# Setting-up moved into the first attention, k ahead of q, output tiles by halves, a bank of its own for the first MLP tile

## Chip, core and metric

One core of one Trainium2 chip. The metric is the time of one execution on the device in microseconds (us), lower is better. An execution's time is its span (first to last instruction, as the profile gives it) plus about 2.0 us. An execution is called fast or slow by its clock and its distance from the fastest; only fast ones are compared. Every execution leaves its span and its mean granted TensorE clock; a full trace is kept of one execution per run.

## The reference

```python
B, H, S, D = 8, 8, 576, 64            # batches, heads, sequence, head width
# attention, per batch and head, two parts that are added:
#   coarse: q, k, v averaged over groups of 4 positions, softmax attention, each row repeated 4 times
#   local:  softmax attention with the mask |i - j| < 4
# x = attention output as (B*S, H*D) = (4608, 512)
h = x @ w_in                          # w_in (512, 2048)
g = 0.5 * h * (1.0 + erf(h / sqrt(2)))
out = g @ w_out                       # w_out (2048, 512), out float32 (4608, 512)
```

## The kernel before

One stream of work per engine: attention of batch 0 in a form of its own (a hand-made order of short steps), then for each of nine chunks of 512 tokens the first MLP product (`m1`), the second (`m2`), and between the second's matmuls the attention of the next batch. `mm()` gives the two PSUM banks `mm0` and `mm1` in turn.

```python
    def load_qk(b):
        for nm, src in (("qn", q), ("kn", k)):
            for c in range(NCK):
                nc.gpsimd.dma_start(
                    out=nat6(ld[b % 2][nm])[:, c, :, :],
                    in_=src[b, :, CH * c:CH * c + CH, :].rearrange("h s d -> s h d"))
                yield
# ... (cut)
    def m1(c):
        g = wpool.tile([128, NJ, 512], F16, tag="gT", bufs=2, name="gT")
        gT[c] = g
        x0 = 512 * c % XR
        if c:
            t = ppool.tile([128, 1024], F32, tag="nm", name="m_first")
            half = [t[:, 0:512], t[:, 512:1024]]
        else:
            half = [mm(), mm()]
        for fcs in ((0, 1, 2), (3,)):
            for j in range(2):
                for fc in fcs:
                    nc.tensor.matmul(out=half[j], lhsT=w_in_sb[:, fc, 128 * j:128 * j + 128],
                                     rhs=xT[:, fc, x0:x0 + 512], start=(fc == 0), stop=(fc == 3))
                    if fc == 3 and c == 0:
                        nc.scalar.activation(out=g[:, j, :], in_=half[j], func=ACTF.Gelu)
                    elif fc == 3 and j == 1:
                        nc.scalar.activation(out=g[:, 0:2, :], in_=t.rearrange("p (j c) -> p j c", j=2), func=ACTF.Gelu)
                    yield
        for j in range(2, NJ):
            ps = mm()
            for fc in range(4):
                nc.tensor.matmul(out=ps, lhsT=w_in_sb[:, fc, 128 * j:128 * j + 128],
                                 rhs=xT[:, fc, x0:x0 + 512], start=(fc == 0), stop=(fc == 3))
                if fc == 3:
                    nc.scalar.activation(out=g[:, j, :], in_=ps, func=ACTF.Gelu)
                yield
# ... m2: for each of four output tiles, 16 matmuls into ps = mm(), then a copy and a store (cut)
    def attn(b, fill):
        fill(6)
        scores(b, 0)
        s_lo(b)
        fill(6)
        mask(0)
        for p in range(NP):
            if p + 1 < NP:
                scores(b, p + 1)
                mask(p + 1)
                fill(2)
            else:
                fill(4)
            av(b, p)
            norm_out(b, p)
            if p + 1 == NP:
                to_gelu()
            else:
                fill(9)
# ... (cut): the attention of batch 0, from the list PLAN0; k, q and v of batch 0 go before all this
    run(load_qk(1))
    vg_load(1, v[1])
    vw_last(1, v[1])
    for f in range(4):
        nc.gpsimd.dma_start(out=w_out_sb[:, 4 * f:4 * f + 4, :],
                            in_=moe_w_out[512 * f:512 * f + 512, :].rearrange("(j p) c -> p j c", p=128))
        vw_load(1, v[1], [f])
    run(load_qk(2))
    first.close()
    ppool = ctx.enter_context(tc.tile_pool(name="psn", bufs=1, space=bass.MemoryType.PSUM, reuse_waits="tile"))
    for i in range(2):
        nc.vector.memset(ld[i]["vd"], 4.0)
        nc.vector.tensor_scalar(out=ld[i]["vlm"][:, :, 64:128], in0=maskL.unsqueeze(2).broadcast_to([128, H, 64]),
                                scalar1=4.0, scalar2=None, op0=ALU.mult)
# ... ON2, BH and ten copies that make `band` (cut)
    for c in range(NCH):
        b = c + 1
        f1 = filler(m1(c)) if c else f1_0
        if b <= 2:
            f1(10)
            for p in range(NP):
                t_in_g(b, p, "k")
                f1(7)
                t_in_g(b, p, "q")
                f1(4)
            k_lo()
            v_down(b)
        if b == 1:
            nc.vector.memset(ld[0]["vw"].rearrange("p j a d -> p (j a d)").bitcast(F32), 0.0)
            v_load(2)
            qk_cast(3)
        elif 2 < b < B:
            prep(b)
        f1()
# ... (cut)
```

The softmax here doesn't subtract the row's maximum and nothing guards it: scores larger than these inputs give would overflow.

Of the kernel before, what the change touches and what calls it, by code (L numbers as in the profile page):

```python
# [9 lines left out]
F32 = mybir.dt.float32  # L10
ACTF = mybir.ActivationFunctionType
ALU = mybir.AluOpType
# [4 lines left out]
def kernel(  # L17
# [9 lines left out]
    nc = tc.nc  # L27
    B, H, S, D = q.shape
    Sd = S // 4
    d_ff = moe_w_in.shape[1]  # L30
    NP = H // 2
# [59 lines left out]
    vlm0 = cpool.tile([128, H, 65], F16, tag="vlm0", name="v_lm0")  # L91
    Gb = cpool.tile([128, 240], F16, tag="Gb", name="Gb")
    GL = cpool.tile([128, 8, 16], F16, tag="GL", name="GL")
    dum = cpool.tile([128, 2], F32, tag="dum", name="dum")
    B0 = cpool.tile([128, 128], F16, tag="B0", name="B0")
    nb = cpool.tile([128, 128], F16, tag="nb", name="nb")
# [10 lines left out]
    def mm():  # L107
        turn[0] ^= 1
        return bank(turn[0])
# [7 lines left out]


    def load_qk(b):
        for nm, src in (("qn", q), ("kn", k)):  # L120
            for c in range(NCK):
                nc.gpsimd.dma_start(  # L122
                    out=nat6(ld[b % 2][nm])[:, c, :, :],
                    in_=src[b, :, CH * c:CH * c + CH, :].rearrange("h s d -> s h d"))
                yield
# [14 lines left out]
    def vg_load(b, src):  # L140
        L = ld[b % 2]
        nc.gpsimd.dma_start(out=L["vt"].rearrange("p h r d -> p h (r d)"),  # L142
                      in_=src[:, 0:512, :].rearrange("h (p r) d -> p h (r d)", r=4))
        nc.gpsimd.dma_start(out=L["vl"].rearrange("p r d -> p (r d)"),
                      in_=src[:, 512:576, :].rearrange("h (p r) d -> h p (r d)", r=4))
# [34 lines left out]
    for t in (kb.rearrange("p a j c -> p (a j c)"), ld[1]["vw"].rearrange("p j a d -> p (j a d)")):  # L180
        nc.scalar.copy(out=t.bitcast(F32).rearrange("p (n c) -> p n c", c=256),
                       in_=zt.bitcast(F32).unsqueeze(1).broadcast_to([128, 10, 256]))
    nc.vector.memset(B0, 1.0)
    nc.vector.memset(Gb, 1.0)
    nc.vector.memset(U, 1.0)
# [41 lines left out]
# [5 lines that stand above are left out]
            t = ppool.tile([128, 1024], F32, tag="nm", name="m_first")  # L232
            half = [t[:, 0:512], t[:, 512:1024]]
        else:
            half = [mm(), mm()]
        for fcs in ((0, 1, 2), (3,)):
            for j in range(2):
                for fc in fcs:
# [15 lines that stand above are left out]

    def m2(c):
        g = gT[c]
        for t in range(4):
            r0 = 512 * c + 128 * t
            if c == NCH - 1 and t == 3:
                for half in range(2):  # L260
                    cs = slice(256 * half, 256 * half + 256)
                    ps = mm()
                    for j in range(NJ):
                        nc.tensor.matmul(out=ps[:, 0:256], lhsT=g[:, j, 128 * t:128 * t + 128],  # L264
                                         rhs=w_out_sb[:, j, cs], start=(j == 0), stop=(j == NJ - 1))
                        yield
                    osb = wpool.tile([128, 512], F32, tag="osb", bufs=5, name="out_sb")[:, 0:256]
                    nc.vector.tensor_copy(out=osb, in_=ps[:, 0:256])  # L268
                    nc.sync.dma_start(out=out[r0:r0 + 128, cs], in_=osb)
                continue  # L270
            ps = mm()
            for j in range(NJ):
                nc.tensor.matmul(out=ps, lhsT=g[:, j, 128 * t:128 * t + 128],  # L273
                                 rhs=w_out_sb[:, j, :], start=(j == 0), stop=(j == NJ - 1))
                if j == NJ - 1:
                    osb = wpool.tile([128, 512], F32, tag="osb", bufs=5, name="out_sb")
                    (nc.vector.tensor_copy if c < NCH - 2 and t < 2 else nc.scalar.copy)(out=osb, in_=ps)  # L277
                    nc.sync.dma_start(out=out[r0:r0 + 128, :], in_=osb)
                yield
# [281 lines left out]
    def spin(n):  # L561
        ps = ppool.tile([128, 512], F32, tag="tr", name="spin")
        for _ in range(n):
            nc.tensor.matmul(out=ps, lhsT=zt[:, 0:128], rhs=zt, start=True, stop=True)



    PLAN0 = """
        Rk0:D Tk0:mm0 Rq0:D Tq0:mm1 KZ10:A NB Rk1:D QD0:A KD00:D QT0:A spin2 Tk1:av Rq1:D KD10:D Tq1:mm1
        KD01:A KZ00:A KZ01:D QT1:A spin1 S0:sc Rk3:D QD1:A Rk2:D KZ11:A Rq3:D Tk2:mm0 E10 KD11:D Tk3:mm1  # L570
        KD12:D E00 KZ12:D E20 Tq3:av KD13:D S1:sc KZ02:A QD3:D Rq2:D KD03:A QT3:D KD02:A E11 Tq2:mm0 KL
        VD:av E21 QD2:D QT2:D E01 S2:sc VLM VDe:A KZ03:D SL:mm0 EL KZ13:D E02 spin2 AV0:av E12 NA0
        AV1:mm0+mm1 E22 spin1 S3:sc NA1 TO0:av E13 XT0:D E23 AV2:mm0+mm1 E03 gelu NA2 TO1:av AV3:sc
        XT1:A NA3 spin1 TO2:av XT2:A spin3 TO3:sc M1A XT3:D M1B
    """
    spin(14)
    f1_0 = filler(m1(0))
    L0 = ld[0]
    slot = {}
# [17 lines left out]
    for word in PLAN0.split():  # L597
# [5 lines left out]
        elif nm == "NB":  # L603
            nc.vector.tensor_scalar(out=nb, in0=B0, scalar1=1.0, scalar2=30000.0,
                                    op0=ALU.subtract, op1=ALU.mult)
        elif nm == "gelu":
            to_gelu()
        elif nm[:2] == "M1":
# [57 lines left out]
            cp(out=xT[:, p, 0:512], in_=half[0])  # L666
            cp(out=xT[:, p, 512:576], in_=half[1][:, 0:64])
    run(load_qk(1))
    vg_load(1, v[1])
    vw_last(1, v[1])  # L670
    for f in range(4):
        nc.gpsimd.dma_start(out=w_out_sb[:, 4 * f:4 * f + 4, :],
                            in_=moe_w_out[512 * f:512 * f + 512, :].rearrange("(j p) c -> p j c", p=128))
        vw_load(1, v[1], [f])
    run(load_qk(2))
    first.close()
    ppool = ctx.enter_context(tc.tile_pool(name="psn", bufs=1, space=bass.MemoryType.PSUM, reuse_waits="tile"))
    for i in range(2):
        nc.vector.memset(ld[i]["vd"], 4.0)
        nc.vector.tensor_scalar(out=ld[i]["vlm"][:, :, 64:128], in0=maskL.unsqueeze(2).broadcast_to([128, H, 64]),  # L680
                                scalar1=4.0, scalar2=None, op0=ALU.mult)
    for hh in range(2):
        r = slice(64 * hh, 64 * hh + 64)
        nc.vector.memset(ON2[r, 64 * hh:64 * hh + 64], 1.0)
        nc.vector.memset(ON2[r, 64 - 64 * hh:128 - 64 * hh], 0.0)
        nc.vector.tensor_copy(out=BH[r, :], in_=B0[r, 64 * hh:64 * hh + 64])
    for j in range(NW):
        x = QN[j] - WN[j]
        nc.vector.tensor_copy(out=band[:, QN[j]:QN[j] + QL[j]], in_=BH[:, x:x + QL[j]])

    for c in range(NCH):
        b = c + 1
        f1 = filler(m1(c)) if c else f1_0
        if b <= 2:
            f1(10)
            for p in range(NP):
                t_in_g(b, p, "k")
                f1(7)
                t_in_g(b, p, "q")
                f1(4)  # L700
            k_lo()
            v_down(b)
        if b == 1:
            nc.vector.memset(ld[0]["vw"].rearrange("p j a d -> p (j a d)").bitcast(F32), 0.0)  # L704
            v_load(2)
            qk_cast(3)
        elif 2 < b < B:
            prep(b)
        f1()
        f2 = filler(m2(c))  # L710
        if b < B:
            to_exp()
            attn(b, f2)
            if b + 2 < B:
                v_load(b + 2)
            if b + 3 < B:
                qk_cast(b + 3)
        f2()
        if b + 2 < B:
            qk_turn(b + 2)  # L720
# [30 lines left out]
```

## Time and profile before

| | before |
|---|---|
| time, four executions | 331.18, 332.15, 329.6, 331.71 us |
| profiled execution: span, granted clock | 330.3 us, 0.995 |
| TensorE (PE) busy | 97% of the span |

The page's rows of busy tenths, 40 slices of 8.26 us each; a 9 is 90% or more:

```profile
PE   8988897999999999999999999999999999999996
DVE  7877677657847944799579957946793660000001
ACT  8745456775688778867886788678868886424710
```

PE loses time only in the first seven slices, which hold the attention of batch 0, the first MLP chunk and the attention of batch 1. The lines that carry the rest are in the prediction below. Two more rows, of the vector engine's (DVE's) timeline, are what the change is to move; the columns are start, length, engine, line, operation, output<-input, shape, count:

```profile
30.52 0.91 DVE L679 MEMSET v_d<- 128x1024 f16 x1 [0.16 <-issue]
53.37 2.19 DVE L704 MEMSET v_win<- 128x2560 f32 x1 [0.48 <-issue]
```

The first opens 4.5 us of setting-up between attention 0 and the first copies of k of batch 1. The second stands ahead of the first mask of batch 1.

### The profile page before, as it was taken

The page shows a single profiled execution, that of the slowest core. Times are in us where ns is not written, and L with a number is a line of the kernel's source. Part 1 is how long each engine was busy: PE and PEld are TensorE (multiplying, and loading weights), DVE is VectorE, ACT ScalarE, POOL GpSimd, SP SyncE. Part 2 cuts the span into 40 slices and gives each one's busy share as a digit, 9 for nine tenths or more (in the row PEclk, how much of TensorE's full clock was granted, in tenths as well). Part 3 has the DMA queues.
Part 4 walks back from the last instruction along what each step waited for, and adds up shares of the span by engine and source line. Part 5 has one row for each costly group of instructions (what it writes and reads, how often), then busy time and mean ns, then how long its engine had stood idle before and what let it go on. Part 6 is the DMA issues. An engine that isn't in the chain of part 4 may idle for free.

```text
span 330.3 us, 6291 instructions
## 1 busy us (share of the span) xinstructions
PE 319.2 (97%) x2526; PEld 172.7 (52%) x2526; DVE 198.5 (60%) x414; ACT 222.6 (67%) x395; POOL 121.7 (37%) x152
## 2 busy tenths in 40 slices
PE   8988897999999999999999999999999999999996
PEld 4864454545565445544554465446545654444444
DVE  7877677657847944799579957946793660000001
ACT  8745456775688778867886788678868886424710
POOL 8966766968372290293039303500000000000000
PEclk9999998999999999999999999999999999999999
DMA  6999999999999999999939994990100010011012
GB/s 82 163 201 156 151 190 160 145 194 145 168 124 192 207 151 154 202 145 172 168 83 129 158 171 113 133 113 32 65 32 0 34 65 32 0 66 64 0 50 80
DMA packets 150973, 38.76 MB, mean 117 GB/s; under 512 B 132896, under 2 KB 146464, under 8 KB 150944
## 3 DMA queue, kind: packets, MB, share of 16 engines
q0 software_dynamic: 122256, 23.02, 86.3%
q1 hardware_dynamic: 28688, 15.34, 22.5%
q8 instruction: 20, 0.33, 0.4%
q14 instruction: 9, 0.07, 0.1%
HBM read 46.01 MB, written 15.34 MB: 186 GB/s over the span
## 4 chain that ended last, share of the span: by engine, by line
PE 86%; POOL 5%; DMA 5%; DVE 2%; issue 1%; POOLq 0%; DVEq 0%
PE m_ps L273 36%; PE m_ps L249 32%; PE m_first L239 4%; DMA w_in_sb<-in_moe_w_in_dram 3%; PE nm L408 3%; PE sc L380 2%; PE sc L398 2%; DMA k_nat<-in_k_dram 1%; POOL old L174 1%; PE nm L405 1%; PE nm L404 1%; PE m_ps L264 1%; PE sc L376 1%; POOL k_nat L122 1%; POOL k_nat L168 1%; DVE v_win L704 1%
## 5 line engine op out<-in xcount | busy, mean ns | idle before, releaser
L273 PE MATMUL m_ps<-w_out_sb,gT 128*128 128x512 f16 x560 | 132.1, 380 | 1.8 <-DMA w_out_sb<-in_moe_w_out_dram 1.8
L249 PE MATMUL m_ps<-xT,w_in_sb 128*128 128x512 f16 x504 | 113.0, 379 | 0.5 <-ACT gT L242 0.5
L252 ACT ACTIVATE gT<-m_ps 128x512 f16<-128x512 f32 x126 | 75.2, 597 | 40.2 <-PE m_ps L249 40.2
L273 PEld LDWEIGHTS <-gT 128*128 128x128 f16 x560 | 51.3, 98 | 55.5 <-issue 3.0
L249 PEld LDWEIGHTS <-w_in_sb 128*128 128x128 f16 x504 | 48.0, 97 | 56.6 <-issue 1.8
L132 POOL DMA_DIRECT2D v_win<-in_v_dram x56 | 44.0, 824 | 19.3 <-DMA v_grp<-in_v_dram 10.0
L423 DVE TENSOR_TENSOR xl<-nm,lr 128x576 f16<-128x576 f32 x28 | 21.2, 758 | 27.0 <-ACT lr L419 27.0
L268 DVE COPY out_sb<-m_ps 128x256 f32<-128x256 f32 x2 | 0.8, 425 | 54.8 <-PE m_ps L264 54.8
L277 ACT COPY out_sb<-m_ps 128x512 f32<-128x512 f32 x21 | 12.3, 586 | 25.1 <-PE m_ps L273 24.9
L392 DVE TENSOR_TENSOR e<-e,band 128x576 f16<-128x576 f16 x28 | 12.5, 450 | 26.6 <-ACT e L387 26.6
L137 POOL DMA_DIRECT2D v_win<-in_v_dram x14 | 9.8, 787 | 48.0 <-PE nm L408 47.6
L435 DVE TENSOR_TENSOR xT<-xl,up 128x576 f16<-128x576 f16 (+8 forms) x41 | 22.1, 566 | 1.0
L417 ACT ACTIVATE lr<-sc 128x576 f32<-128x576 f32 x28 | 18.4, 658 | 2.5 <-PE sc L398 2.5
L418 ACT ACTIVATE lr<-lr 128x576 f32<-128x576 f32 x28 | 19.1, 683 | 0.9
L386 ACT ACTIVATE ed<-sc 128x288 f16<-128x288 f32 x28 | 11.4, 406 | 11.4 <-PE sc L380 11.4
L387 ACT ACTIVATE e<-sc 128x576 f16<-128x576 f32 x28 | 18.0, 644 | 0.0
L425 DVE TENSOR_TENSOR up<-nm,lr 64x144 f16<-64x144 f32 x56 | 16.5, 295 | 0.4
L239 PE MATMUL m_first<-xT,w_in_sb 128*128 128x512 f16 x64 | 15.1, 379 | 0.0
L244 ACT ACTIVATE gT<-m_first 128x1024 f16<-128x1024 f32 x8 | 8.2, 1024 | 8.7 <-PE m_first L239 8.7
L155 POOL DMA_DIRECT2D q<-in_q_dram x5 | 13.9, 2782 | 0.0
L142 POOL DMA_DIRECT2D v_grp<-in_v_dram x7 | 9.5, 1351 | 10.9 <-DVE v_two L350 10.9
L420 ACT ACTIVATE lr<-lr 64x288 f32<-64x288 f32 x28 | 12.4, 443 | 0.9
(186 smaller groups left out, 470.5 us busy)
## 6 DMA issues: line engine op xcount, KB each, us to landing
out_dram<-out_sb SPq DMA_DIRECT2D x35, 256.0 KB, 2.4
v_win<-in_v_dram POOLq DMA_DIRECT2D x56, 72.0 KB, 8.0
v_grp<-in_v_dram POOLq DMA_DIRECT2D x7, 512.0 KB, 11.1
k<-in_k_dram POOLq DMA_DIRECT2D x5, 576.0 KB, 12.5
q<-in_q_dram POOLq DMA_DIRECT2D x5, 576.0 KB, 15.0
w_in_sb<-in_moe_w_in_dram POOLq DMA_DIRECT2D x4, 512.0 KB, 8.6
w_out_sb<-in_moe_w_out_dram POOLq DMA_DIRECT2D x4, 512.0 KB, 9.5
q_nat<-in_q_dram POOLq DMA_DIRECT2D x12, 96.0 KB, 8.4
```

The source lines that it names most:

```text
L132: nc.gpsimd.dma_start(out=vw[64 * hh:64 * hh + 64, 0:9, p, 64 * hh:64 * hh + 64], in_=bass.AP(x.tensor, x.offset, [[D, 64], [57 * D, 9], [ ...
L155: nc.gpsimd.dma_start(out=t, in_=src[b].rearrange("h s d -> s h d"))
L239: nc.tensor.matmul(out=half[j], lhsT=w_in_sb[:, fc, 128 * j:128 * j + 128], rhs=xT[:, fc, x0:x0 + 512], start=(fc == 0), stop=(fc == 3))
L249: nc.tensor.matmul(out=ps, lhsT=w_in_sb[:, fc, 128 * j:128 * j + 128], rhs=xT[:, fc, x0:x0 + 512], start=(fc == 0), stop=(fc == 3))
L252: nc.scalar.activation(out=g[:, j, :], in_=ps, func=ACTF.Gelu)
L273: nc.tensor.matmul(out=ps, lhsT=g[:, j, 128 * t:128 * t + 128], rhs=w_out_sb[:, j, :], start=(j == 0), stop=(j == NJ - 1))
L387: nc.scalar.activation(out=e.rearrange("p (g c) -> p g c", g=2), in_=sc2[:, :, 0:SH], func=ACTF.Exp, scale=0.125)
L417: nc.scalar.activation(out=lr2, in_=sc2[:, :, 0:SH], func=ACTF.Ln)
L418: nc.scalar.activation(out=lr2, in_=lr2, func=ACTF.Exp, scale=-1.0)
L423: nc.vector.tensor_tensor(out=xl.rearrange("p (g c) -> p g c", g=2), in0=nm2[:, :, 0:SH], in1=lr2, op=ALU.mult)
L425: nc.vector.tensor_tensor(out=up[64 * hh:64 * hh + 64, :], in0=nm2[0:64, hh, SH:SH + Sd], in1=lrd[:, Sd * hh:Sd * hh + Sd], op=ALU.mult)
L435: nc.vector.tensor_tensor(out=xT[:, p, y:y + z - a].rearrange("p (g r) -> p g r", r=4), in0=xl[:, a:z].rearrange("p (g r) -> p g r", r=4), ...
```

## The change

The intent: take work and waits out of the stretch from 29 to 72 us. k of batch 1 is loaded and turned before q; constants are made in gaps of attention 0; the first MLP tile no longer shares a bank with the third; the first two output tiles are each summed in two halves, so that the last quarters of `w_out` are wanted later, and `w_out` is put earlier among the loads. The words `I0` to `I5` in the list PLAN0 are the moved pieces of setting-up. The core of the diff (cut: the tile `four` and its memset, the dispatch of the `I` words, the body of `warm`):

```diff
     def load_qk(b):
-        for nm, src in (("qn", q), ("kn", k)):
+        for nm, src in (("kn", k), ("qn", q)):
             for c in range(NCK):
@@ m1 @@
-            half = [mm(), mm()]
+            half = [ppool.tile([128, 512], F32, tag="tr", name="m_first"), mm()]
@@ m2 @@
     def m2(c):
         g = gT[c]
+        pair = [mm(), mm()] if c == 0 else []
+        if c == 0:
+            for t in range(2):
+                for j in range(NJ // 2):
+                    nc.tensor.matmul(out=pair[t], lhsT=g[:, j, 128 * t:128 * t + 128],
+                                     rhs=w_out_sb[:, j, :], start=(j == 0), stop=False)
+                    yield
         for t in range(4):
             r0 = 512 * c + 128 * t
-            ps = mm()
-            for j in range(NJ):
+            ps = pair.pop(0) if pair else mm()
+            for j in range(NJ // 2 if c == 0 and t < 2 else 0, NJ):
@@ attention 0 @@
+    def init(i):
+        if i < 2:
+            L = ld[1 - i]
+            nc.scalar.copy(out=L["vd"][:, :, 64:128], in_=four.unsqueeze(2).broadcast_to([128, H, 64]))
+            nc.scalar.activation(out=L["vlm"][:, :, 64:128], in_=maskL.unsqueeze(2).broadcast_to([128, H, 64]),
+                                 func=ACTF.Copy, scale=4.0)
+        elif i < 4:
+            t = ld[0]["vw"][:, 5 * i - 10:5 * i - 5].rearrange("p j a d -> p (j a d)")
+            nc.scalar.copy(out=t.bitcast(F32).rearrange("p (n c) -> p n c", c=256),
+                           in_=zt.bitcast(F32).unsqueeze(1).broadcast_to([128, 5, 256]))
+        elif i == 4:
+            for hh in range(2):
+                r = slice(64 * hh, 64 * hh + 64)
+                nc.vector.memset(ON2[r, 64 * hh:64 * hh + 64], 1.0)
+                nc.vector.memset(ON2[r, 64 - 64 * hh:128 - 64 * hh], 0.0)
+                nc.vector.tensor_copy(out=BH[r, :], in_=B0[r, 64 * hh:64 * hh + 64])
+        else:
+            for j in range(NW):
+                x = QN[j] - WN[j]
+                nc.vector.tensor_copy(out=band[:, QN[j]:QN[j] + QL[j]], in_=BH[:, x:x + QL[j]])
@@ PLAN0, the lines with an I word as they are after @@
+        KD01:A KZ00:A KZ01:D QT1:A spin1 S0:sc Rk3:D QD1:A Rk2:D KZ11:A Rq3:D Tk2:mm0 E10 I4 KD11:D Tk3:mm1
+        KD12:D E00 KZ12:D E20 I0 Tq3:av KD13:D S1:sc KZ02:A QD3:D Rq2:D KD03:A QT3:D KD02:A E11 Tq2:mm0 KL
+        VD:av E21 I1 QD2:D QT2:D E01 S2:sc VLM VDe:A KZ03:D SL:mm0 EL KZ13:D E02 spin2 AV0:av E12 NA0
+        AV1:mm0+mm1 E22 I2 spin1 S3:sc NA1 TO0:av E13 XT0:D E23 AV2:mm0+mm1 E03 gelu NA2 TO1:av AV3:sc
+        XT1:A NA3 I5 spin1 TO2:av XT2:A I3 spin3 TO3:sc M1A XT3:D M1B
-    spin(14)
+    spin(10)
+    warm()          # 40 small matmuls on zeros, into a bank of their own
@@ loads and set-up after attention 0 @@
-    vg_load(1, v[1])
-    vw_last(1, v[1])
     for f in range(4):
         nc.gpsimd.dma_start(out=w_out_sb[:, 4 * f:4 * f + 4, :],
                             in_=moe_w_out[512 * f:512 * f + 512, :].rearrange("(j p) c -> p j c", p=128))
-        vw_load(1, v[1], [f])
+        if f == 0:
+            vg_load(1, v[1])
+        elif f == 1:
+            vw_last(1, v[1])
+            vw_load(1, v[1], [0])
+        else:
+            vw_load(1, v[1], [f - 1])
+    vw_load(1, v[1], [3])
     run(load_qk(2))
     first.close()
     ppool = ctx.enter_context(tc.tile_pool(name="psn", bufs=1, space=bass.MemoryType.PSUM, reuse_waits="tile"))
-    for i in range(2):
-        nc.vector.memset(ld[i]["vd"], 4.0)
-        nc.vector.tensor_scalar(out=ld[i]["vlm"][:, :, 64:128], in0=maskL.unsqueeze(2).broadcast_to([128, H, 64]),
-                                scalar1=4.0, scalar2=None, op0=ALU.mult)
-    for hh in range(2):
-        r = slice(64 * hh, 64 * hh + 64)
-        nc.vector.memset(ON2[r, 64 * hh:64 * hh + 64], 1.0)
-        nc.vector.memset(ON2[r, 64 - 64 * hh:128 - 64 * hh], 0.0)
-        nc.vector.tensor_copy(out=BH[r, :], in_=B0[r, 64 * hh:64 * hh + 64])
-    for j in range(NW):
-        x = QN[j] - WN[j]
-        nc.vector.tensor_copy(out=band[:, QN[j]:QN[j] + QL[j]], in_=BH[:, x:x + QL[j]])
 
     for c in range(NCH):
         b = c + 1
         f1 = filler(m1(c)) if c else f1_0
         if b <= 2:
             f1(10)
-            for p in range(NP):
-                t_in_g(b, p, "k")
-                f1(7)
-                t_in_g(b, p, "q")
-                f1(4)
+            for i, w in enumerate("k0 k1 q0 k2 q1 k3 q2 q3".split()):
+                t_in_g(b, int(w[1]), w[0])
+                f1(7 if i % 2 == 0 else 4)
             k_lo()
             v_down(b)
         if b == 1:
-            nc.vector.memset(ld[0]["vw"].rearrange("p j a d -> p (j a d)").bitcast(F32), 0.0)
             v_load(2)
             qk_cast(3)
         elif 2 < b < B:

```

More of the change, by code (lines that the diff above doesn't have):

```diff
@@ L93 @@
     GL = cpool.tile([128, 8, 16], F16, tag="GL", name="GL")
+    four = cpool.tile([128, H], F32, tag="four", name="four")
     dum = cpool.tile([128, 2], F32, tag="dum", name="dum")
@@ L182 @@
                        in_=zt.bitcast(F32).unsqueeze(1).broadcast_to([128, 10, 256]))
+    nc.vector.memset(four, 4.0)
     nc.vector.memset(B0, 1.0)
@@ new lines, in warm, with tiles @@
+    def warm():
+        t = ppool.tile([128, 1536], F32, tag="sc", name="warm")
+        def tiles(n, kw, mw, qs, o):
+            for i in range(n):
+                for a, b in qs:
+                    nc.tensor.matmul(out=t[b:b + mw, 512 * (a // 64) + o * (i % 4):512 * (a // 64) + o * (i % 4) + o],
+                                     lhsT=zt[a:a + kw, 0:mw], rhs=zt[a:a + kw, 0:o], start=True, stop=True)
+        tiles(4, 64, 64, ((0, 0), (0, 64), (64, 0), (64, 64)), 58)
+        tiles(4, 64, 128, ((0, 0), (64, 0)), 58)
+        tiles(2, 64, 128, ((0, 0), (64, 0)), 120)
+        tiles(4, 64, 64, ((0, 0), (64, 64)), 58)
+        tiles(1, 64, 64, ((0, 0), (0, 64), (64, 0), (64, 64)), 288)
@@ L568 @@
     PLAN0 = """
         Rk0:D Tk0:mm0 Rq0:D Tq0:mm1 KZ10:A NB Rk1:D QD0:A KD00:D QT0:A spin2 Tk1:av Rq1:D KD10:D Tq1:mm1
-        KD01:A KZ00:A KZ01:D QT1:A spin1 S0:sc Rk3:D QD1:A Rk2:D KZ11:A Rq3:D Tk2:mm0 E10 KD11:D Tk3:mm1
-        KD12:D E00 KZ12:D E20 Tq3:av KD13:D S1:sc KZ02:A QD3:D Rq2:D KD03:A QT3:D KD02:A E11 Tq2:mm0 KL
-        VD:av E21 QD2:D QT2:D E01 S2:sc VLM VDe:A KZ03:D SL:mm0 EL KZ13:D E02 spin2 AV0:av E12 NA0
-        AV1:mm0+mm1 E22 spin1 S3:sc NA1 TO0:av E13 XT0:D E23 AV2:mm0+mm1 E03 gelu NA2 TO1:av AV3:sc
@@ L574 @@
-        XT1:A NA3 spin1 TO2:av XT2:A spin3 TO3:sc M1A XT3:D M1B
-    """
-    spin(14)
+        KD01:A KZ00:A KZ01:D QT1:A spin1 S0:sc Rk3:D QD1:A Rk2:D KZ11:A Rq3:D Tk2:mm0 E10 I4 KD11:D Tk3:mm1
+        KD12:D E00 KZ12:D E20 I0 Tq3:av KD13:D S1:sc KZ02:A QD3:D Rq2:D KD03:A QT3:D KD02:A E11 Tq2:mm0 KL
+        VD:av E21 I1 QD2:D QT2:D E01 S2:sc VLM VDe:A KZ03:D SL:mm0 EL KZ13:D E02 spin2 AV0:av E12 NA0
+        AV1:mm0+mm1 E22 I2 spin1 S3:sc NA1 TO0:av E13 XT0:D E23 AV2:mm0+mm1 E03 gelu NA2 TO1:av AV3:sc
@@ L605 @@
                                     op0=ALU.subtract, op1=ALU.mult)
+        elif nm[0] == "I":
+            init(int(nm[1]))
         elif nm == "gelu":
```

## The prediction

> **What bounds the kernel now.** I read the busy row of 40 slices first: PE is at 9 nearly everywhere, and only the first seven slices (58 us) have 8s and an occasional 7. Next the chain of work that ended last, for its first 100 us: it leaves PE in one stretch only, before 60 us.
>
> ```profile
> 16.48 11.50 DMA w_in_sb<-in_moe_w_in_dram
> ...
> 31.59 4.67 DMA k_nat<-in_k_dram
> ...
> 53.37 2.19 DVE v_win L704
> 55.56 0.32 DVE e L392
> ```
>
> (Start, length, what.) From 57 us on every piece is PE, so time saved before then moves the end by the same amount, as long as the loads of later batches keep up. PE's own timeline tells where it stood still; the bracket is idle time before the row and what ended it.
>
> ```profile
> 17.74 0.38 PE L324 MATMUL av<-old,Gb 112*128 112x512 f16 x1 [0.69 <-DMA old<-in_v_dram]
> 18.52 0.38 PE L324 MATMUL av<-old,Gb 128*128 128x512 f16 x1 [0.40 <-DMA old<-in_v_dram]
> ...
> 31.69 2.32 PE L249 MATMUL m_ps<-xT,w_in_sb 128*128 128x512 f16 x10 [0.47 <-ACT gT L242]
> 33.85 0.21 PE L307 MATMUL tg_k<-I,k_nat 96*128 96x96 f16 x1
> 34.30 0.22 PE L307 MATMUL tg_k<-I,k_nat 96*128 96x96 f16 x1 [0.24 <-DMA k_nat<-in_k_dram]
> ...
> 36.31 0.22 PE L307 MATMUL tg_k<-I,k_nat 96*128 96x96 f16 x1 [0.43 <-DMA k_nat<-in_k_dram]
> ...
> 54.91 0.59 PE L273 MATMUL m_ps<-w_out_sb,gT 128*128 128x512 f16 x2 [1.79 <-DMA w_out_sb<-in_moe_w_out_dram]
> 55.92 0.64 PE L398 MATMUL sc<-e,ON 128*128 128x288 f16 x2 [0.42 <-DVE e L392]
> ```
>
> The reader sees four losses: 0.47 us for a PSUM bank that gelu still reads, about 2.2 us in transposes that follow k chunk by chunk, 1.79 us for the last quarter of w_out, 0.42 us for the masked exponentials. The stretches by engine show a fifth:
>
> ```profile
> 50.00:55.00 5.00, 3.21 (x39) 2.06 (x38) 4.38 (x8) 3.55 (x8) 2.63 (x4) 1.00 1.84 177
> 55.00:60.00 5.00, 4.58 (x27) 2.40 (x27) 2.76 (x7) 2.18 (x4) 4.85 (x7) 0.66 1.94 124
> ```
>
> The third number from the end is the granted clock: 0.66 over 5 us, after PE was busy only 3.21 us of the five before. That is 5 x 0.34 = 1.7 us of lost work.
>
> [...] 512 KB of w_out landed in 9.5 us, a 72 KB v_win in 8.0 us, so all wait in one backlog and moving a load only permutes landings.
>
> **Part 1: k ahead of q.** The issues (section of DMA issues, narrowed to one issue at a time) landed thus: the six first loads, q now, at 28.5 to 32.0 us, the six second ones, k now, at 33.7 to 36.3. Exchanging them puts all of k at 32.0 and q at 36.3. PE reaches the first k transpose at 33.85 (33.5 with part 2), when k is there. In the new order (k0, k1, q0, ...) q0 is reached 0.4 + 1.52 + 0.4 + 0.88 = 3.2 us later (transposes, 7 matmuls, transposes, 4 matmuls at 0.216), at 36.7, 0.4 us after the last q. So no wait is left. Before, the seven matmuls after k0 began at 36.51; now at 33.5 + 0.4 = 33.9. **Gain 2.6 us**, part 2 included. DVE keeps up: four k at 1.8 us and four q at 0.7 us are 10.0 us of copies in a stretch of 12.8 us.
>
> **Part 2: own bank for the first MLP tile.** Its third tile no longer waits 0.47 us, but the fourth now wants the bank of the second tile, whose gelu ends at 32.14, while it could start at 31.92: 0.25 us stay. Net 0.2 to 0.35 us, already counted in the 33.5. Without part 1 it would be worth nothing, since k would still land at 36.3.
>
> **Part 3: setting-up moved.** Removed from DVE after attention 0: two memsets of 0.91, two maskings of 0.5 and 0.6, the ON2/BH pieces and ten band copies, 30.5 to 35.0 us. Before, they lay under the wait for k; with part 1 alone they would delay the first k copies by about 1 us, so they have to go. Also removed: the 2.19 us memset of v_win, which does lie on the path, between v_lm and the first mask. Added in attention 0, where ACT waits 1.18, 2.89, 1.38 and 2.18 us and DVE 1.37 us near the end: on ACT four copies of 512 columns (0.6 each, as the casts of that width) and two zero fills of half the 2.31 us (1.16 each), 4.7 us in four lumps of 1.2; on DVE 0.6 and 0.93 us. The one on DVE holds up the third transposes by about 0.5 us, and the second ACT lump puts the exponentials that free the scores bank at 18.8 instead of 17.1. Both are swallowed by the 0.69 + 0.40 us that PE waits for v of batch 0: it cannot pass 18.52 in either kernel. The same holds for the start: four spins fewer, 40 small matmuls more, at 0.03 to 0.05 us each (the 65-column rows go every 0.03) perhaps 0.5 us late at 6.3, caught up by 11.9, where PE waited 0.52 for a load. **Attention 0: 0, give or take 0.3 us**; the MLP still starts at 29.3.
>
> **Part 4: output tiles by halves, w_out loads earlier.** With the first MLP ended at 46.7 instead of 49.29, PE walks 6 output matmuls, scores and low scores, 6 more, scores, 2 more (0.42 + 0.25 + 0.42 + 14 x 0.216) and is at 50.85. DVE finishes the last q at 46.2, KL and the v sums (4.0 us, was 48.86 to 52.88) at 50.3, and, the memset gone, the mask at 50.7: the 0.42 us wait is gone. Attention's products take 0.78, and nine output matmuls follow. The last quarter of w_out was wanted by matmul 13; it is now the 21st, at about 52.9. Its landing is the question. Before: 54.9. The backlog ahead of it holds the same loads except one pair of v_win, worth 1.2 us (four pairs and quarters between 43.7 and 54.9, 3.7 us each, of which the last pair alone 1.3): **53.7. So 0.8 us of the 1.79 stay.** [...]
>
> **The sum.** From the end of the first MLP to the next MLP's first matmul: 49.29 to 72.10 now, 22.8 us; the same stretch for the next batch, undisturbed: 89.33 to about 108.0, 18.7 us. So 4.1 us are to be had (1.7 clock, 1.8 w_out, 0.4 mask, small change), and 3.3 are taken if w_out still costs 0.8. With 2.6: **5.9 us**. From there on the order of work changes only for k and q of batch 2, which landed by about 64 and are wanted at 68. Later loads have room too: GpSimd waited 47.6 us in four times for PE to release v_win (list of waits). 331.2 - 5.9 = **325.3 us**.
>
> **Rivals.** (a) **w_out comes as late as before, or the clock falls again.** For: DMA is at 9 in every slice here and total bytes are unchanged. If it lands at 54.9, 1.2 us more are lost, and with a half-speed window 1.7 more: 326.5 to 328.2. Against: it is one pair further ahead[...]. (b) **w_out is no bound any more**, because the loads now begin with a plain large one and fill the trough in DMA around 35 us: the full 6.7 us, 324.5, just at 2%. (c) **Setting-up holds up attention 0.** ACT gets 4.7 us in a stage that is a chain of short steps; if two lumps of 1.2 us land on it, MLP 0 starts up to 1.5 us late and the gain shrinks to about 4.5: 326.7. Against: the ACT waits named. (d) **A later load becomes the bound** when PE is 6 us earlier. The 13.6 us longest wait of GpSimd for PE speaks against it; it would leave 328 to 331.
>
> **Range and chances.** The sum is 5.9, with 0.6 us from w_out, 0.3 from attention 0, and the spread of the runs (329.6 to 332.15). The largest gain I can name is 6.7, against 6.6 for 2%: faster by over 2% needs (b) or a lucky draw, 0.27. Slower has no mechanism: 0.02. Range 323.4 to 328.4.
>
> **What would show it.** First k transposes at 33.5 with no DMA in the bracket; first MLP over at 46.7; no memset before the mask; one wait of 0.3 to 1.5 us for w_out near 53; clock 1.00 from 5 us on; the next MLP at 66 to 67 instead of 72.1; the MLP's start still at 29.3. Wrong if the MLP starts after 30, if q0 or v_win brings a new wait, or if a later batch waits for DMA.

## The result, and the profile after

| | before | after |
|---|---|---|
| time, four executions | 331.18, 332.15, 329.6, 331.71 us | 326.59, 327.82, 328.19, 326.91 us |
| median | 331.44 us | 327.37 us |
| profiled execution: span, clock | 330.3 us, 0.995 | 324.5 us, 1.000 |

The ratio is 0.9886, with a 95% interval of 0.9837 to 0.9935. A ratio is the mean time of one kernel's fast executions over that of the other's of the same rounds, so it is not quite the ratio of the medians. The time lies inside the stated range, 2 us above the stated value. The two profiled executions differ by 5.8 us, almost exactly the 5.9 of the sum; the timed ones by 3.8 in the mean. That gap is what the experiments are about.

First the profile of after, PE's timeline (bracket: idle before the row, and what ended it):

```profile
18.61 0.38 PE L333 MATMUL av<-old,Gb 128*128 128x512 f16 x1 [0.17 <-DMA old<-in_v_dram]
...
31.40 2.58 PE L251 MATMUL m_ps<-xT,w_in_sb 128*128 128x512 f16 x10
33.81 0.42 PE L316 MATMUL tg_k<-I,k_nat 96*128 96x96 f16 x6
...
34.22 1.67 PE L251 MATMUL m_ps<-xT,w_in_sb 128*128 128x512 f16 x7
...
51.10 0.41 PE L407 MATMUL sc<-e,ON 128*128 128x288 f16 x2
...
52.32 1.83 PE L282 MATMUL m_ps<-w_out_sb,gT 128*128 128x512 f16 x7
...
66.01 1.89 PE L241 MATMUL m_first<-xT,w_in_sb 128*128 128x512 f16 x8
```

None of the four waits of before is left: the third MLP tile, all six k transposes in one piece, the first masked product, and the seven matmuls that take in the last quarter of `w_out` have no bracket. The next MLP begins at 66.01 instead of 72.10. The stretches by engine (stretch and length, then busy time and number of instructions of PE, its weight loads, DVE, ACT and POOL, then the granted clock, third from the end, and the DMA):

```profile
50.00:55.00 5.00, 5.00 (x57) 3.06 (x56) 2.81 (x7) 3.77 (x10) 3.71 (x5) 1.00 1.96 172
55.00:60.00 5.00, 5.00 (x59) 3.14 (x58) 4.32 (x9) 4.42 (x10) 5.00 (x8) 1.00 1.93 164
```

PE is busy throughout, and the half-speed window (a clock of 0.50 from 55.5 to 58.9 us in before's trace) is gone. But the first row above shows what had been eaten: PE used to wait 0.69 + 0.40 us for v of batch 0, and now waits 0.17. Attention 0 has hardly any slack left, and the last quarter of `w_out` landed at 46.2 + 7.1 = 53.3 us, when PE wanted it at 52.32 + 4 x 0.216 = 53.2. This execution ran between two limits without touching either.

### The profile page after: what moved, and what is told of

Read it like the earlier page. It is cut to its first block, busy times and chain, and to the rows that moved or that the text cites. A ratio compares the mean times of both kernels' runs of the same rounds, so it can differ in the third digit from the quotient of the medians.

```text
span 324.5 us, 6382 instructions
## 1 busy us (share of the span) xinstructions
PE 317.1 (98%) x2562; PEld 171.8 (53%) x2562; DVE 190.2 (59%) x410; ACT 226.7 (70%) x401; POOL 121.1 (37%) x152
## 4 chain that ended last, share of the span: by engine, by line
PE 92%; DMA 2%; ACT 2%; POOL 1%; DVE 1%; issue 0%; POOLq 0%; DVEq 0%
PE m_ps L282 36%; PE m_ps L251 33%; PE m_first L241 5%; PE sc L389 2%; PE nm L417 2%; DMA q_nat<-in_q_dram 2%; PE sc L407 2%; PE sc L385 1%; PE m_ps L273 1%; PE nm L413 1%; PE nm L414 1%; PE m_ps L263 1%; POOL k_nat L169 1%; PE tg_k L316 1%; PE tg_q L316 1%; PE sl L373 1%
## 5 line engine op out<-in xcount | busy, mean ns | idle before, releaser
L282 PE MATMUL m_ps<-w_out_sb,gT 128*128 128x512 f16 x544 | 127.6, 379 | 0.0
L282 PEld LDWEIGHTS <-gT 128*128 128x128 f16 x544 | 49.6, 97 | 52.0 <-issue 0.3
L401 DVE TENSOR_TENSOR e<-e,band 128x576 f16<-128x576 f16 x28 | 12.7, 453 | 30.7 <-ACT e L396 30.7
L241 PE MATMUL m_first<-xT,w_in_sb 128*128 128x512 f16 x68 | 16.3, 379 | 0.0
L429 ACT ACTIVATE lr<-lr 64x288 f32<-64x288 f32 x28 | 12.4, 443 | 0.9
L307 DVE TENSOR_REDUCE qd<-q_nat 128x576 f16<-128x2304 f16 x5 | 12.8, 2553 | 0.2
## 6 DMA issues: line engine op xcount, KB each, us to landing
v_grp<-in_v_dram POOLq DMA_DIRECT2D x7, 512.0 KB, 12.7
```

Of the source, the lines that this page charges most:

```text
L282: nc.tensor.matmul(out=ps, lhsT=g[:, j, 128 * t:128 * t + 128], rhs=w_out_sb[:, j, :], start=(j == 0), stop=(j == NJ - 1))
```

## The experiments

Twelve runs were made, in four calls, each call on one chip beside the kernel before. The table has the ratio to before; "full clock" counts the fast executions with a mean granted clock of 0.998 or more. A half-speed window as in before's trace (3.4 us at a clock of 0.50, from 55.5 to 58.9 us) or in a_third's (0.99 over 10 to 15 us and 0.67 over 15 to 20) takes 1.7 of 330 us and brings the mean to 0.995, so these are the executions without one. The last two columns are from each run's one trace: when the first MLP began (the end of attention 0) and when the last quarter of `w_out` landed (issue plus time to landing).

| run | ratio to before | 95% interval | mean span, us | full clock | MLP 0 from | w_out landed |
|---|---|---|---|---|---|---|
| before, first profile | 1 | | | | 29.33 | 54.9 |
| b_again | 1.0020 | 0.9972 to 1.0067 | 330.0 | 0 of 6 | 29.60 | 55.6 |
| changed, first profile | 0.9886 | 0.9837 to 0.9935 | 325.3 | 3 of 4 | 29.67 | 53.3 |
| a_again (changed) | 0.9936 | 0.9881 to 0.9990 | 326.9 | 2 of 6 | 29.03 | 56.8 |
| a_third (changed) | 0.9907 | 0.9876 to 0.9938 | 326.0 | 1 of 6 | 31.45 | 54.5 |
| only_setup | 0.9999 | 0.9955 to 1.0044 | 328.8 | 2 of 6 | 30.12 | 54.2 |
| only_halves | 0.9937 | 0.9894 to 0.9981 | 328.2 | 5 of 6 | 29.23 | 55.1 |
| no_kfirst | 0.9902 | 0.9872 to 0.9933 | 325.7 | 5 of 6 | 29.37 | 54.5 |
| no_setup | 0.9952 | 0.9919 to 0.9985 | 327.2 | 3 of 6 | 29.20 | 53.9 |
| no_halves | 1.0013 | 0.9979 to 1.0048 | 329.4 | 0 of 6 | 31.78 | 53.8 |
| no_wearly | 0.9903 | 0.9876 to 0.9930 | 325.8 | 3 of 6 | 31.29 | 54.7 |
| w3_early | 0.9918 | 0.9868 to 0.9969 | 326.4 | 3 of 6 | 32.88 | 54.6 |
| init_late | 0.9856 | 0.9812 to 0.9899 | 325.3 | 6 of 6 | 28.64 | 53.0 |
| best | 0.9834 | 0.9797 to 0.9871 | 323.7 | 5 of 5 | 29.60 | 51.9 |

The fast executions of before beside these had full clock in 17 of 43 (6 of 10, 4 of 11, 3 of 11 and 4 of 11 by call; a slow one is left out): mean span 328.3 us, the other 26 330.3. In three calls its mean fast span was 329.2 or 329.3, in that of only_halves and init_late 330.2, so about 1 us of the gain of these two is the draw of before. In only_setup, no_kfirst and no_setup, time minus span was 2.2 to 2.4 us, in the other runs 1.9 to 2.2; no run explains it, and it makes their ratios look up to 0.3 us worse than their spans. `best` had one slow execution (330.4 us of span, clock 0.979), left out.

### The same kernels again: a_again, b_again, a_third

The kernels are unaltered.

> The changed kernel unaltered, once more. The profiled pair of runs differs by 5.8 us of span, the timed runs by 3.8 us in the mean. Theory A (the removed waits are worth 5.8 to 6, and the timed difference is run-to-run spread: the kernel before sometimes escapes its half-speed window of 1.7 us, the changed one sometimes still waits for the last quarter of w_out, which landed at 53.3 us when PE wanted it at about 53.2): spans spread from 324.5 to about 327, mean 325.3, several with a granted clock of 0.995, and a profile that shows either no wait or a w_out wait of up to 1.5 us. Rival B (the profile of the changed kernel was typical, and something outside the span costs time): spans all at 324.5 to 324.8, and time minus span over 2.5 us instead of 2.0.

> The kernel before, as a kernel of its own. Theory A: its spans spread from 327.6 to 330.3, about 1.7 us apart according to whether a half-speed window falls on the wait for w_out, so its mean is about 1 us below the profiled 330.3. Rival: all at 329 to 330 with the same clock 0.995.

Theory A's spread was there, and larger than it said. a_again's spans went from 325.6 to 330.4, time minus span stayed near 2.1 us, and rival B falls. The traced execution of a_again, PE's timeline and stretches:

```profile
56.81 1.44 PE L282 MATMUL m_ps<-w_out_sb,gT 128*128 128x512 f16 x3 [4.11 <-DMA w_out_sb<-in_moe_w_out_dram]
```

```profile
50.00:55.00 5.00, 2.70 (x31) 1.54 (x28) 2.50 (x6) 3.03 (x6) 3.44 (x5) 1.00 1.64 164
55.00:60.00 5.00, 3.19 (x19) 1.71 (x19) 0.01 (x1) 0.95 (x2) 2.95 (x4) 0.52 1.34 85
```

The same kernel, the same loads, and the quarter landed 3.5 us later than in the first profile, cost 4.11 us of waiting and then the clock (0.52 over 55 to 60 us). So its arrival is a draw, not a time. For before, theory A was half wrong: b_again's spans went from 328.8 to 331.7 and none of its six had full clock, but of the executions of before over all calls 17 of 43 did. So about six in ten executions of before lose time to a half-speed window.

> The changed kernel again, beside the candidate. From its ten executions so far: mean span 326.3, about a third with a half-speed window; 3 to 4 us below before of the same rounds. Its profile should show the kdz wait of the third k part (0.2 us or more) and either a w_out wait or none.

Mean 326.0 as expected. Its trace shows a second place for the half-speed window, in attention 0. Stretches, then PE, then DVE:

```profile
10.00:15.00 5.00, 3.95 (x75) 3.53 (x72) 3.82 (x14) 4.69 (x10) 4.86 (x10) 0.99 2.42 155
15.00:20.00 5.00, 5.00 (x58) 4.51 (x55) 3.60 (x9) 2.48 (x6) 5.00 (x8) 0.67 1.72 191
```

```profile
14.79 0.56 PE L668 MATMUL av<-I,q_nat 72*128 72x72 f16 x8 [0.29 <-DVE kdz L680]
```

```profile
13.88 0.52 DVE L592 COPY BH<-B 64x64 f16<-64x64 f16 x1
14.43 0.31 DVE L680 CAST kdz<-av 64x144 f16<-64x144 f32 x1
```

The BH piece of the setting-up stands directly ahead of the `kdz` cast (it copies averaged k out of PSUM) that frees the bank for the q transposes. The clock fell at about 15 (0.67 over 15 to 20 us), the first MLP began at 31.45, and so the `w_out` quarter, at 54.5, found PE late as well and cost nothing. One loss hid the other.

### Single parts: only_setup, only_halves

```diff
 only_setup:  before + init(), four, the I words; - the block after attention 0, - the v_win memset
 only_halves: before + the two hunks of m2
```

> The kernel before with the setting-up alone moved into the attention of batch 0. My step: k still lands at 36.3 us, so the first MLP gains nothing and attention 0 is about 0.3 us later; the 2.19 us memset is gone before the first mask, so the 0.42 us wait for it goes, but the 1.79 us wait for w_out stays as it is. Expected 0.1 to 0.8 us faster than before, with the half-speed window still there. Rival (the memset was the bound of the output stage): 2 us or more faster.

No gain by the ratio (0.9999), just under my step's range; 0.5 us by mean spans, inside it; neither is clear of the noise. The mechanism is there: the profile has no wait for the mask and still waits 1.52 us for `w_out` at 54.28. The half-speed window that I expected did not fall in the traced execution (clock 0.999), but four of the six did not have full clock. The rival falls.

> The kernel before with the first two output tiles by halves and nothing else. Undoing the halves alone gave back the whole gain (mean span 329.4, before 329.3), so theory C says: the bound of the output stage of batch 0 is the landing of the last quarter of w_out, and only moving the demand for it helps. Then this kernel, whose demand moves from matmul 13 to 21, has no w_out wait, no half-speed window around 55, but the memset's wait before the first mask (about 2 us at 53.5 to 55.5) stays: mean span 327 to 328, 1.5 to 2.3 us under before. If each part were worth its own share (theory A), it gains 1.8 us for w_out plus up to 1.7 us clock: about 326. If the halves help only together with the moved memset: 329.

Measured 0.63% or about 2.1 us, with a mean span of 328.2: theory C, though about 1 us of it is the draw of before in this call. Its PE timeline waits in one place of the output stage, and not for `w_out`:

```profile
54.93 0.41 PE L405 MATMUL sc<-e,ON 128*128 128x288 f16 x2 [2.06 <-DVE e L399]
```

The memset's wait is as expected, the quarter landed at 55.1 and was not waited for, and five of six executions kept the full clock (before in the same call: 3 of 11). Most of this gain is the clock: executions with full clock alone average 327.9 us here and 328.3 in before, since the wait for the memset has taken the place of the one for `w_out`. Why 2.06 us of waiting here left the clock at 1.00 (50 to 60 us), when 1.79 us in before was followed by 0.50 at 55.5, no run shows.

### One part undone: no_kfirst, no_setup, no_halves, no_wearly

```diff
 no_kfirst: - k0 k1 q0 ... and ("kn", k) first      + k0 q0 k1 q1 ... and ("qn", q) first
 no_setup:  - the I words                           + the block after attention 0, + the v_win memset
 no_halves: - pair, - the eight matmuls ahead       + 16 matmuls per tile
 no_wearly: - w_out, vg, w_out, vw_last, vw0 ...    + vg, vw_last, w_out, vw0, w_out, vw1 ...
```

> The changed kernel with q loaded ahead of k again, and turned k0 q0 k1 q1. My step: the k transposes wait for the load again, the seven matmuls after them begin at about 36.4 instead of 34.2 us, the first MLP ends 2 to 2.6 us later, and w_out is then no longer waited for, so against the changed kernel's mean (about 326.2 of span, 3.0 to 3.8 us below before) 1 to 2.5 us are lost, less where the w_out wait had been eating the gain. Rival (w_out alone decides when the output stage goes on, so the earlier MLP only waits longer): no loss at all against the changed kernel's mean.

0.9902 against 0.9886, 0.9936 and 0.9907 for the changed kernel: nothing is lost, as the rival said. The mechanism of my step is there all the same. PE's timeline:

```profile
34.54 0.22 PE L316 MATMUL tg_k<-I,k_nat 96*128 96x96 f16 x1 [0.54 <-DMA k_nat<-in_k_dram]
35.08 0.22 PE L316 MATMUL tg_k<-I,k_nat 96*128 96x96 f16 x1 [0.32 <-DMA k_nat<-in_k_dram]
36.40 0.22 PE L316 MATMUL tg_k<-I,k_nat 96*128 96x96 f16 x1 [1.10 <-DMA k_nat<-in_k_dram]
```

The first MLP took from 29.37 to 49.39, 20.0 us, against 29.67 to 47.01, 17.3 us, in the changed kernel. But the quarter of `w_out` then comes, at 54.5, before it is wanted, and five of six executions had full clock. My reading is that what k first saves is saved ahead of a transfer that does not come sooner, so that the mean gives it back. That is argued, not shown: with full clock alone the mean spans are 325.7 here and 325.4 in the changed kernel.

> The changed kernel with the setting-up back after attention 0 and the v_win memset back ahead of the first mask. My step: the 4.5 us of vector work from 30.9 us on holds up the first k copies by about 1 us and the memset the first mask by 2 us or more, so the first masked product starts at about 54 instead of 51.1: 2 to 3 us lost. Attention 0 gets back 0.3 us or, where the first loads are late, up to 1 us. Rival (w_out decides): less than 1 us lost, because the memset lies under the wait for w_out.

About 1.4 us lost against the mean of the three changed ratios (0.991), between the two answers. By spans it is less: 2.1 us under before of the same call, where a_again and a_third are 2.4 and 3.1 under. So the loss in the mean is not clear of the noise. The wait is where my step put it:

```profile
53.91 0.41 PE L407 MATMUL sc<-e,ON 128*128 128x288 f16 x2 [2.35 <-DVE e L401]
```

That costs 2.35 us in the output stage, and attention 0, at 29.20, gives part of it back. The clock stayed at 1.00 through this wait (50 to 60 us).

> The changed kernel with whole output tiles in turn, loads as in the change. The last quarter of w_out is then wanted by matmul 13 instead of 21, at about 50.7 us, and lands at 53.3 to 56.8: the profile shows a w_out wait of 2.5 us or more, a half-speed window follows in most executions, and 2.5 to 4 us are lost: about the time of before. Rival (halves buy nothing, the loads only need to be early): within 0.7 us of the changed kernel.

The whole gain is lost: 1.0013, no execution with full clock. The predicted wait of 2.5 us is only 0.92 in this trace, because attention 0 was late there (first MLP from 31.78, with a half-speed window at 15.4 us, 0.66 over 15 to 20). The halves are the part on which the rest depends.

> The changed kernel with the loads of v and w_out in the order of before, halves kept. In before the last quarter of w_out was issued at 44.7 to 45.9 and landed at 54.2 to 55.6; in the change it was issued later, 46.2 to 47.4, since an issue waits for the landing of the load eight before it, which is now a large one, and landed at 53.3 to 56.8. If the reordering moved the landing, this kernel waits 1 to 2 us for w_out at about 53 us in its profile and is 0.5 to 1.5 us slower than the changed kernel. If it moved nothing, as the issue times suggest, both have the same mean within 0.7 us.

No loss: the reordering bought nothing. Over the traces, the quarter landed at 54.9, 55.6, 54.2, 55.1 and 54.7 in the order of before (mean 54.9), and at 53.3, 56.8, 54.5, 54.5, 53.9, 53.8 and 53.0 in the order of the change (mean 54.3). It is issued later, 45.6 to 47.4 instead of 44.7 to 45.9. In both first traces no load up to 70 us is issued before the one eight places ahead has landed; in the new order that one is a whole quarter of `w_out`, which in the first profile landed at 45.9, and the last quarter was issued at 46.19.

### Further kernels: w3_early, init_late, best

```diff
 w3_early:  loads ... vw0, w_out 2, w_out 3, vw1, vw2, vw3  (was: w_out 2, vw1, w_out 3, vw2, vw3)
 init_late: PLAN0  - E10 I4 KD11     + E10 KD11
                   - E21 I1 QD2 QT2 E01   + E21 QD2 QT2 E01 I1
                   - NA3 I5          + NA3 I4 I5
 best:      both, and w_in's fourth quarter issued after k and ahead of q of batch 1
```

> The changed kernel with the third and fourth quarter of w_out both issued ahead of the second pair of v_win. If its spread comes from the last quarter of w_out arriving within a few tenths of when PE wants it, that quarter lands 1 us or more earlier, no profile shows a w_out wait, and the mean time falls by 0.5 to 1 us against the changed kernel of the same rounds, with a smaller spread. If the spread comes from elsewhere: same mean and spread. If the second pair of v_win now comes late (wanted at about 55.3): up to 1 us slower.

0.9918, no better than the changed kernel, and the quarter landed at 54.6. Its traced execution (mean clock 0.994) began the first MLP at 32.88, after waits in attention 0 and a half-speed window at 16.6 us. The run sent me to attention 0.

> The changed kernel with two pieces of setting-up moved to other gaps of attention 0: the ON2 and BH pieces on the vector engine from before the third k part to after the last normalisation, the second pair of v_d and v_lm fills on the scalar engine to behind the exponentials that free the scores bank. Theory D: in the changed kernel those pieces lie on the path whenever the first loads land late (last first-batch q at 12.9 to 14.1 us in the profiles), which makes attention 0 late by 0.3 to 3.4 us and lets a half-speed window fall at 15 to 20 us. Then no profile row of the transposes waits over 0.3 us for the kdz copies, the first MLP starts at 29.3 to 30, and the mean span is 0.3 to 1 us lower than the changed kernel's 326.3. If w_out's landing decides anyway: same mean, with a w_out wait of 1 us or more in its place.

Theory D is borne out. All six executions had full clock, and the ratio is 0.9856. The gain over the changed kernel is about 1.8 us by ratios (0.991 - 0.9856, times 331), but 0.9 by mean spans (325.3 against 326.2 over its 16 executions, none of them in this call). It lies in the clock: the six changed executions with full clock average 325.4. In the traces of the eight kernels with the pieces where the change put them, attention 0 ended at 29.67, 29.03, 31.45, 30.12, 29.37, 31.78, 31.29 and 32.88; in the six without them or with them later, at 29.33, 29.60, 29.23, 29.20, 28.64 and 29.60. `no_setup`, `init_late` and `best` keep the 40 small warming matmuls, so those are not the cause. A half-speed window falls in attention 0 in four of the eight (a_third 0.67, no_halves and no_wearly 0.66 over 15 to 20 us, w3_early 0.994 over its whole execution; the first MLP from 31.9 on average) and in none of the six; the other four of the eight average 29.5. So nearly all of the lateness comes with the clock.

The rival is that the first loads were merely late in those four. They were: the last q of batch 0 landed at 13.1 to 14.1 there, at 12.4 to 12.7 in five of the six. But in the sixth, no_setup, it landed at 13.7, as in no_wearly. The third q transposes, then 15 to 20 us, of no_setup (first and third row) and no_wearly (second and fourth):

```profile
14.54 0.42 PE L666 MATMUL av<-I,q_nat 72*128 72x72 f16 x8 [0.18 <-DVE kdz L678]
15.20 0.42 PE L668 MATMUL av<-I,q_nat 72*128 72x72 f16 x8 [0.83 <-DVE kdz L680]
15.00:20.00 5.00, 4.91 (x75) 4.01 (x73) 4.43 (x12) 2.65 (x7) 5.00 (x8) 1.00 1.67 189
15.00:20.00 5.00, 4.80 (x57) 4.56 (x57) 3.69 (x11) 2.63 (x7) 5.00 (x8) 0.66 1.56 176
```

Late loads with the pieces made attention 0 late here, late loads alone did not. That is one pair, and only_setup, with the pieces and a landing at 13.6, kept the clock (first MLP from 30.12). What is left in this kernel's trace is `w_out`, PE's timeline:

```profile
53.12 0.81 PE L282 MATMUL m_ps<-w_out_sb,gT 128*128 128x512 f16 x3 [0.44 <-DMA w_out_sb<-in_moe_w_out_dram]
```

> The changed kernel with the two pieces of setting-up moved as in init_late, the third and fourth quarter of w_out both ahead of the second pair of v_win, and the fourth quarter of w_in issued between k and q of batch 1 rather than ahead of both. The last is meant to keep the DMA engines full around 31 to 36 us, where small loads are issued one by one every 0.77 us. If the landing of the last w_out quarter is the remaining bound (theory C), it lands at 51.5 to 53 in place of 53 to 56.8, no execution waits for it, and the mean span falls to 324.3 to 324.8, 0.5 to 1 us under init_late and 1.5 to 2 under the changed kernel of the same rounds. If q, now behind 512 KB more, lands after 37 us, PE waits there instead and the mean is that of init_late or worse. If nothing but the loads' own spread is left: 325.3.

The quarter landed at 51.9, in the stated range, q was there (its last part at 36.9), and no row of the output stage waits. Mean fast span 323.7, 2.4 us under the changed kernel of the same rounds and 5.5 under before: ratio 0.9834. PE's timeline of this kernel at the place of the old wait:

```profile
52.24 1.67 PE L282 MATMUL m_ps<-w_out_sb,gT 128*128 128x512 f16 x7
```

It beats both kernels, also among executions with full clock alone (323.7 against 325.4 in the changed kernel). How much is due to `w_in`'s move and how much to the order of `w_out` was not separated.

## Why the prediction was right or wrong

**The time** was inside the range, and the mechanism of most steps was right, but the closeness of 5.9 to the 5.8 us between the two profiles is luck. Up to the end of the first MLP 2.3 us came instead of 2.6, from there to the next MLP 3.8 instead of 3.3, because this execution had no wait for `w_out`; and a_again, the same kernel, was traced at 330.4 us, no less than before's 330.3. For the mean the sum was too large.

**Part 1, 2.6 us:** the seven matmuls after k0 began at 34.22 instead of 36.51, 2.3 us, and 2.6 less the 0.34 us by which attention 0 was late is just that. The mechanism was right. Its worth was not: `no_kfirst` shows that the mean time does not need it. The step took a gain ahead of the `w_out` wait as additive to it.

**Part 2:** the third tile starts without a wait, as said. No run isolates it.

**Part 3, "Attention 0: 0, give or take 0.3 us": this step failed.** In the first profile it was 0.34 us late; over eight traces with the pieces so placed the first MLP began at 30.7 on average, over six others at 29.3, so 1.4 us. I set the lengths of the pieces against the gaps of one execution. In the eight traces the DVE piece took 0.7 to 1.2 us instead of 0.6, the third transposes waited 0.2 to 1.5 us for the `kdz` cast behind it, and in four of the five in which the first loads came late as well (13.1 us or later) the clock fell to half (0.66 or 0.67 over 15 to 20 us in a_third, no_halves and no_wearly). My own sign of being wrong, an MLP that starts after 30, came true in a_third (31.45). This is rival (c), which I had argued away with those very gaps. That the memset had to go was right as a wait (2.06 and 2.35 us where it stays beside the halves); its worth in the mean is not clear of the noise.

**Part 4, "0.8 us of the 1.79 stay":** none in the first profile, 4.11 in a_again, none in a_third, 0.44 in init_late. The landing at 53.7 was a fair mean (54.3 measured) and a poor number, since three executions of one kernel span 3.5 us. That w_out lands earlier by being ahead of one pair of v_win was wrong in its working: the mean moved by 0.6 us instead of 1.2. The gain is the later demand, as `no_halves` and `only_halves` show.

**The sum, "1.7 clock":** mis-sized. The 1.7 us were in the execution profiled; 17 of 43 fast executions of before have none of it, so it is worth about 1.0 us in the mean. And the sum was subtracted from the median of executions of which some never had that loss. The changed kernel has full clock in 6 of 16 executions, no more often than before: the window that left the `w_out` wait came back in attention 0 (0.67 over 15 to 20 us in a_third) or at a late `w_out` (0.52 over 55 to 60 in a_again). So in the mean this term came to about nothing, and what the removed waits are worth by themselves is the difference with full clock, 328.3 - 325.4 = 2.9 us, where the sum without the clock had 4.2. After the fact, with the clock at 1.0 and attention 0 at -1.4 (its lost clock included), the sum of 5.9 becomes 3.8, beside 2.1 to 3.8 measured in three runs; that is a reckoning and no test. init_late, which takes away the second term, gains 4.8 by its ratio, about 1 us of it the draw of before.

Idle time by itself does not say when the clock falls. In before's trace it went to 0.50 at 55.5 us, after 1.79 us of waiting for `w_out` that ended at 54.91; in a_third's it fell at about 15 us (0.99 over 10 to 15, 0.67 over 15 to 20), after PE had been busy 3.95 of those first 5 us; in a_again's it was 0.52 over 55 to 60 us, with a wait of 4.11 us that ended at 56.81. 2.06 us of waiting in only_halves and 2.35 us in no_setup left it at 1.00. That the clock would stay at 1.00 through the 0.8 us of the sum was my estimate; the nearest case is init_late, with 0.44 us of waiting and 1.00 over 50 to 60 us.

What stays open: in how many of the changed kernel's executions the half-speed window fell in attention 0 and in how many at `w_out` (one trace per run), why no_kfirst, with the same attention 0, had it in only one of six, and what decides whether a wait of about 2 us takes the clock along.

## What to carry to other kernels

Size a gap from several executions before filling it: work moved into a gap of one profile may be on the path in the next, above all ahead of a step that frees a buffer. When a transfer's arrival is the bound and varies by microseconds, move its demand and not only its issue, and do not add gains that lie ahead of it to the sum. A loss that only some executions have, such as a clock window (26 of 43 fast executions of before), enters the sum with its share.
